# A first search in three rounds in place of four, with 128 thresholds in the first and their comparisons on GpSimd

## The chip, the core and the metric

The kernel runs on one core of a Trainium2 chip. The engines are TensorE (PE, and PEld for its weight loads), VectorE (DVE), ScalarE (ACT), GpSimd (POOL) and SyncE (SP, which issues DMAs here). Each takes its instructions in the order of the program, and they wait for each other by semaphores. The metric is the device time of one execution in microseconds (us), the median of several runs.

## The reference, cut to what matters

Pooled attention (keys and values are means over 8 tokens), then a mixture of eight experts in which each expert takes at most `cap` = 576 of the 4608 tokens, given out in the order of the gate logits over all pairs of token and expert.

```python
scores = scale * np.matmul(q, k_p.transpose(0, 1, 3, 2))      # k_p, v_p: means over 8
attn = softmax(scores)
x = (attn @ v_p)                                              # as 4608 tokens x 512
logits = x @ w_gate                                           # 8 experts
for idx in np.argsort(-logits.flatten()):
    tok, e = idx // E, idx % E
    if assigned[tok] >= 0 or counts[e] >= cap:
        continue
    assigned[tok] = e
    counts[e] += 1
for e in range(E):
    out[assigned == e] = np.maximum(x[assigned == e] @ w1[e], 0) @ w2[e]
```

## The kernel before

The 4608 tokens are 36 tiles of 128 (`NC` = 36, one token in each partition). Three stages follow each other.

**Attention** (`Attention.run`) loops over the tiles with a pipeline: iteration n makes the score products of tile n (`st_s`), turns the weights of tile n - 1 (`st_e`), multiplies tile n - 2 with the values (`st_av`), and on DVE takes the maximum of tile n (`top`), subtracts it (`softmax`, ACT then takes the exponent), and normalises tile n - 3 (`norm`). The bank of the score products is there once, so the score products of tile n + 1 wait for the subtraction of tile n. The gate logits come out of the same value products (`gates`): every fourth `norm` adds the heads of four tiles into `lg` with one longer reduction. A batch has 4.5 tiles; two iterations in each batch have a `prep_v` and a `prep_g` more. GpSimd pools k and v of batches 1 to 7 (`pool_k`, `pool_v`). `after[i]` is a list of steps that are put behind norm(i), in iteration i + 3; all queues keep the written order. `finish` takes the last three tiles; its `next(after)` calls run `Routing.begin`, which handles the last logits and starts the search.

**Routing** (`Routing`) finds for each of eight phases the expert that fills up next and its tokens. Each token has a best logit `bv` and a one-hot `oh` of its expert. A search narrows a threshold: a round compares the place of every token's best logit with `J` = 32 levels, PE counts for each level and expert how many tokens lie above (36 products of 128 x 8, where four tiles of 32 columns share the weights), DVE tests whether a count is over `cap`, and a product with ones gives every partition the number of levels (`up`), from which the next, 28.4 times finer, places follow. The first search (`search_first`) has four rounds. Its range comes from `bounds`, from the first 24 tiles: per partition a maximum and a minimum, a transpose, a product, and seven small DVE instructions; `best(0, 28)`, `levels`, `place` and the first comparisons follow in iterations 31 to 35. `wanted` gives each token its expert's number in the shadow of the later rounds. `close` makes the expert's number (`eid`) and the row numbers (`rows`) out of the last vote.

**Experts** (`experts`): SP loads the weights of expert `eid`, POOL gathers its rows of x by indirect DMA, ACT and DVE cut both into a high and a low part, PE multiplies. The later searches are laid between these products by due times written into the code. `warm` keeps PE busy with products of ones before the first expert. `wake` is an indirect DMA with no use for its result. If an exact count was missed, `suspect` sets a flag, and all experts run a second time.

Of the kernel before, what the change touches and what calls it, by code (L numbers as in the profile page):

```python
# [9 lines left out]
F32 = mybir.dt.float32  # L10
# [13 lines left out]
class Attention:  # L24
# [44 lines left out]
    def local(self, loc, full, consts, more, then):  # L69
# [12 lines left out]
        n = 0  # L82
# [32 lines left out]
        more()  # L115
# [89 lines left out]
    def prep_g(self, b):  # L205
# [10 lines left out]
        return put  # L216

# [113 lines left out]
    def run(self, ctx, full, consts, more, after, end, warm):  # L331
# [37 lines left out]
        self.local(ctx.enter_context(tc.tile_pool(name="loc", bufs=1)), full, consts, more, first_k)  # L369
# [10 lines left out]
        for n in range(nt):  # L380
# [42 lines left out]
class Routing:  # L423
# [25 lines left out]
    def consts(self, jp, ident):  # L449
# [10 lines left out]
        self.jrow = cst.tile([128, J], F16, name="jrow")  # L460
# [20 lines left out]
        nc.gpsimd.tensor_scalar(self.untri, self.tri, -31.0, None, op0=OP.mult)  # L481
        self.spread = cst.tile([128, 224], F16, name="spread")
# [6 lines left out]
    def more(self):  # L489
# [14 lines left out]
        self.q2 = cst.tile([128, NC, 2], F16, name="q2a")  # L504
        self.cmp = cst.tile([128, NC + 3, J], BF, name="cmp")
        self.thr = cst.tile([128, J], F32, name="thr")
        self.lg0 = cst.tile([128, NC, 8], F32, name="lg0")
        self.lo0 = cst.tile([128, 1], F32, name="lo0")
# [5 lines left out]
    def before_search(self, n):  # L514
# [6 lines left out]
        else:  # L521
            for g in self.g0:
                nc.scalar.activation(g[:1], self.ones[:1, :16], AF.Copy, scale=-1.0 - EDGE)
            nc.scalar.activation(self.jrow, self.i36[:, :self.J], AF.Copy)
# [18 lines left out]
    def bounds(self, wk, cols):  # L543

        nc = self.nc
        lg = self.lg[:, :cols].rearrange("p c e -> p (c e)")
        mm = wk.tile([128, 2], F32, name="mm")
        nc.vector.tensor_reduce(mm[:, 0:1], lg, axis=AX.X, op=OP.max)
        nc.vector.tensor_reduce(mm[:, 1:2], lg, axis=AX.X, op=OP.min)
        nc.vector.tensor_scalar(mm[:, 1:2], mm[:, 1:2], -1.0, None, op0=OP.mult)  # L550
        yield
        ps = self.psum()
        nc.tensor.transpose(ps[:2, :128], mm, self.ident)
        m2 = wk.tile([2, 1], F32, name="m2")
        nc.vector.tensor_reduce(m2, ps[:2, :128], axis=AX.X, op=OP.max)
        d2 = wk.tile([2, 2], F32, name="d2")
        nc.vector.tensor_scalar(d2, self.ident[:2, :2], m2, None, op0=OP.mult)
        one = wk.tile([2, 128], F32, name="one2")
        nc.vector.memset(one, 1.0)
        yield  # L560
        ps = self.psum()
        nc.tensor.matmul(ps[:, :2], one, d2, start=True, stop=True)
        b = wk.tile([128, 3], F32, name="b2")
        nc.vector.tensor_copy(b[:, :2], ps[:, :2])

        nc.vector.tensor_tensor(b[:, 2:3], b[:, 0:1], b[:, 1:2], op=OP.add)
        nc.vector.scalar_tensor_tensor(self.hi, b[:, 2:3], 0.125, b[:, 0:1], op0=OP.mult, op1=OP.add)
        nc.vector.scalar_tensor_tensor(self.lo0, b[:, 2:3], -0.125, b[:, 1:2], op0=OP.mult, op1=OP.subtract)
        self.ranges()
# [6 lines left out]
    def place(self, c0, c1):  # L576

        if c0 == 0:
            self.q32 = self.wk.tile([128, self.NC], F32, name="q32")
        self.nc.vector.tensor_scalar(self.q32[:, c0:c1], self.bv[:, c0:c1], self.lo0, self.scale, op0=OP.subtract,  # L580
                                     op1=OP.mult)

    def one(self, c):

        nc = self.nc
# [5 lines left out]
    def best(self, c0=0, c1=None):  # L591
# [3 lines left out]
        if c0 == 0:  # L595
            n = self.n = 1 - getattr(self, "n", 1)
            self.bv, self.oh = self.bvs[n], self.ohs[n]
# [1051 lines left out]
```

## Time and profile before

| | |
|---|---|
| median of three runs | 596.1 us (595.87 to 596.28) |
| profiled execution, its own time | 595.69 us |
| its span, first to last instruction | 593.9 us |
| PE busy | 572.0 us (96%) |
| DVE busy | 392.6 us (66%) |
| ACT busy | 304.7 us (51%) |
| POOL busy | 180.4 us (30%) |
| mean granted clock of PE | 0.983 |

The times of the rows are microseconds from the start of the span. "Busy" is the union of an engine's instructions. Matmul ends are modelled, so a PE that shows 100% need not be at its peak; a row's idle time is that of its engine just before it, with what ended it. Spans on POOL are rough.

### The profile page before, as it was taken

To read this page: it belongs to the slowest core of one execution; us is meant where nothing else is said; L and a number is where in the kernel's file an instruction comes from. 1 tells how busy PE (TensorE), PEld (TensorE's weight loads), DVE (VectorE), ACT (ScalarE), POOL (GpSimd) and SP (SyncE) were. 2 spreads that over 40 slices of the span, in tenths; PEclk is the share of its full clock that TensorE was granted. 3 is DMA by queue.
4 is the path that set the end of the run, shared out by engine and by line. 5 is a ranking of instruction groups with operands and counts; after the bars stand their busy time and mean duration, and the time that the engine had idled before them with its cause. 6 is when DMAs were issued, how large, how long until landed. Compare 5 with 4: busy or idle time off the path is not lost.

```text
span 593.9 us, 11073 instructions
## 1 busy us (share of the span) xinstructions
PE 572.0 (96%) x4045; PEld 506.9 (85%) x4045; DVE 392.6 (66%) x1139; ACT 304.7 (51%) x631; POOL 180.4 (30%) x235
## 2 busy tenths in 40 slices
PE   7999999995999999999999999999999999999993
PEld 4999999993897799779978987997899899889972
DVE  8677887997886778668766876586487346416200
ACT  6444444452551385376745584285549627935210
POOL 3999999200200410330222121112221212210021
PEclk9999999995999999999999999999999999999997
DMA  8999982113541763547538337543833653350010
GB/s 347 419 424 420 423 309 90 72 72 113 165 143 37 256 196 130 136 108 293 98 97 283 102 79 224 165 108 74 273 124 81 200 190 89 89 195 12 2 58 26
DMA packets 64016, 99.83 MB, mean 168 GB/s; under 512 B 34752, under 2 KB 34768, under 8 KB 61392
## 3 DMA queue, kind: packets, MB, share of 16 engines
q1 hardware_dynamic: 52704, 70.66, 35.3%
q0 software_dynamic: 5920, 18.89, 10.0%
q10 hardware_dynamic: 5328, 9.48, 4.2%
q8 instruction: 34, 0.56, 0.4%
q14 instruction: 30, 0.25, 0.1%
HBM read 72.40 MB, written 18.87 MB: 154 GB/s over the span
## 4 chain that ended last, share of the span: by engine, by line
PE 85%; issue 7%; DVE 4%; DMA 2%; POOL 1%; ACT 0%; another core or an unknown queue 0%; POOLq 0%; SPq 0%; ACTq 0%; DVEq 0%
PE h L1215 32%; PE h L1251 27%; PE psa L269 7%; PE pss L224 6%; PE h L1256 4%; PE pse L256 2%; PE rt L256 1%; DMA rawq<-in_q_dram 1%; PE rt L662 1%; DMA out_dram<-yt,rows 1%; PE rt L210 1%; PE rt L714 1%; DVE e L238 1%; PE h L535 1%; PE tp L1188 1%
## 5 line engine op out<-in xcount | busy, mean ns | idle before, releaser
L1251 PE MATMUL h<-w2h,hh 128*128 128x512 f32 x256 | 101.9, 398 | 0.3 <-PEq L1332 0.3
L1251 PE MATMUL h<-w2h,hl 128*128 128x512 f32 x256 | 101.3, 396 | 0.0
L1251 PE MATMUL h<-w2l,hh 128*128 128x512 f32 x256 | 101.0, 394 | 0.0
L1231 POOL DMA_INDIRECT out_dram<-yt,rows x36 | 38.0, 1056 | 195.9 <-ACT yt L1271 170.0
L1220 ACT ACTIVATE hh<-h 128x256 fp32r<-128x256 f32 (+2 forms) x129 | 52.6, 409 | 83.6 <-PE h L1215 83.2
L1215 PE MATMUL h<-xh,w1h 128*128 128x256 f32 (+2 forms) x516 | 93.4, 299 | 0.2 <-ACT xh L1190 0.2
L1215 PE MATMUL h<-xl,w1h 128*128 128x256 f32 (+2 forms) x516 | 91.9, 298 | 0.0
L1215 PE MATMUL h<-xh,w1l 128*128 128x256 f32 (+2 forms) x516 | 90.6, 296 | 0.0
L1215 PEld LDWEIGHTS h<-xh,w1h 128*128 128x128 f32 x516 | 76.9, 189 | 1.2 <-ACT xh L1190 0.5
L1215 PEld LDWEIGHTS h<-xl,w1h 128*128 128x128 f32 x516 | 76.3, 190 | 0.1
L1215 PEld LDWEIGHTS h<-xh,w1l 128*128 128x128 f32 x516 | 76.1, 189 | 0.0
L1119 POOL DMA_INDIRECT xa<-xd,rows x33 | 33.3, 1009 | 135.3 <-ACT xg L1142 38.8
L1225 DVE SCALAR_TENSOR_TENSOR hl<-h,hh 128x256 fp32r<-128x256 f32 (+2 forms) x129 | 56.8, 448 | 21.5 <-ACT hl L1223 10.9
L1271 ACT ACTIVATE yt<-h 128x512 f32<-128x512 f32 x32 | 19.1, 597 | 93.5 <-PE h L1251 79.9
L269 PE MATMUL psa<-vblk,eT 128*128 128x146 f32 (+3 forms) x390 | 59.2, 302 | 0.1
L1251 PEld LDWEIGHTS h<-w2h,hh 128*128 128x128 f32 x256 | 48.2, 188 | 9.3 <-issue 0.7
L1251 PEld LDWEIGHTS h<-w2l,hh 128*128 128x128 f32 x256 | 48.2, 188 | 9.2
L1251 PEld LDWEIGHTS h<-w2h,hl 128*128 128x128 f32 x256 | 48.3, 189 | 8.4
L1168 DVE TENSOR_TENSOR w1l<-raw,w1h 128x512 fp32r<-128x512 f32 x64 | 42.0, 686 | 17.7 <-ACT w1h L1164 17.5
L269 PEld LDWEIGHTS psa<-vblk,eT 128*128 128x128 f32 (+1 forms) x390 | 50.7, 179 | 1.5 <-issue 0.3
L1177 DVE TENSOR_TENSOR w2l<-raw,w2h 128x512 fp32r<-128x512 f32 x64 | 43.2, 682 | 3.4 <-ACT w2h L1174 3.1
L224 PE MATMUL pss<-kblk,rawq 128*128 128x144 f32 (+1 forms) x320 | 43.4, 293 | 1.9 <-PE psa L201 0.9
(253 smaller groups left out, 942.9 us busy)
## 6 DMA issues: line engine op xcount, KB each, us to landing
raw<-in_moe_w_dram SPq DMA_DIRECT2D x64, 512.0 KB, 6.0
xd<-xt ACTq DMA_DIRECT2D x36, 256.0 KB, 6.2
rawv<-in_v_dram SPq DMA_DIRECT2D x7, 1280.0 KB, 12.8
rawk<-in_k_dram SPq DMA_DIRECT2D x7, 1152.0 KB, 12.7
rawq<-in_q_dram SPq DMA_DIRECT2D x6, 1152.0 KB, 11.9
rawq<-in_q_dram SPq DMA_DIRECT2D x2, 640.0 KB, 11.0
rawk<-in_k_dram SPq DMA_DIRECT2D x2, 576.0 KB, 3.9
rawq<-in_q_dram SPq DMA_DIRECT2D x2, 512.0 KB, 6.2
```

What stands on the lines that cost most here:

```text
L224: nc.tensor.matmul(ps[cols, j // 2, 144 * (j % 2):144 * (j % 2) + 144], self.q_of(b, j, n, cols.stop - cols.start), self.kblk[b % 4][:, j] ...
L269: self.nc.tensor.matmul(o[h], self.eT[i][:, c, h], self.vblk[b % 4][:, self.BLOCKS[c]:self.BLOCKS[c + 1]], start=(c == cs[0]), stop=(c == ...
L1119: self.nc.gpsimd.indirect_dma_start(out=to[:n], out_offset=None, in_=self.xd, in_offset=bass.IndirectOffsetOnAxis(ap=rows[:n, t:t + 1], ax ...
L1168: self.nc.vector.tensor_tensor(l, raw, h.bitcast(F32), op=OP.subtract)
L1177: self.nc.vector.tensor_tensor(self.w2l[:, i], self.raw2[e][:, i], self.w2h[:, i].bitcast(F32), op=OP.subtract)
L1215: nc.tensor.matmul(ps[:, :m], a[:, j, fs], b[:, j, o], start=(n == 0), stop=(n == 11))
L1220: nc.scalar.activation(hh[:, f, o], ps[:, :m], AF.Relu)
L1225: later(0.65, 0.4, lambda f=f, o=o, m=m, ps=ps: nc.vector.scalar_tensor_tensor(hl[:, f, o], ps[:, :m], 0.0, hh[:, f, o].bitcast(F32), op0= ...
L1231: st = nc.gpsimd.indirect_dma_start(out=rows, out_offset=bass.IndirectOffsetOnAxis(ap=idx, axis=0), in_=y, in_offset=None)
L1251: nc.tensor.matmul(ps, a[:, f, o], b[:, f], start=(f == 0 and k == 0), stop=(f == 7 and k == 2))
L1256: nc.tensor.matmul(ps, self.hl[:, f, 512:], b[:, f], start=(f == 0 and k == 0), stop=(f == 7 and k == 1))
L1271: self.nc.scalar.activation(y, ps, AF.Copy)
```

## The change

- **Range** (`mix`, `range_of`): from the first 16 tiles, out of the largest logit, the smallest and the smallest best logit. A 4 x 7 matrix of constants (built on GpSimd in `more`) gives, by one product, the lower ends, the three step sizes and the places' origin at once; ACT makes the copies. Its steps stand behind norm(15), norm(16), norm(18) and norm(27), its transpose and its product behind the score products of iterations 20 and 24 (`mid`).
- **First round with 128 thresholds**: `thr` holds 128 levels. GpSimd compares 32 tiles, one `tensor_scalar` of 128 columns for each (`compare`), into a tile in one of the four buffers of `rawq` (`room`), and makes the one-hot rows of these tiles (`fresh`, 8 columns each), the places of 32 tiles (`place`) and the products with the expert numbers (`wish`). DVE takes the best logits of these tiles (`top_of`), and all of the last four tiles (`late_tiles`).
- **Rounds 2 and 3** are as before, with 32 levels; the fourth is gone. `wanted` is no longer run for the first search: the last four tiles of `wish` go under the second round, the reduction under the third.
- `wake` and `levels` (now on GpSimd) stand behind norm(22), the comparisons behind norm(23), norm(27) and norm(31).

```diff
-    def run(self, ctx, full, consts, more, after, end, warm):
+    def run(self, ctx, R, consts, more, after, mid, end, warm):
...
             if n in behind:
                 behind[n]()
+            for f in mid.get(n, ()):
+                f()
...
-        self.jrow = cst.tile([128, J], F16, name="jrow")
+        self.jrow = cst.tile([128, 128], F16, name="jrow")
...
+        nc.gpsimd.tensor_scalar(self.jrow, jp, self.pcol, None, op0=OP.add)
...
+    def mix(self, loc):
...
+        sh = [0.3125 * (J * SHRINK) ** -i / J for i in range(3)]
...
+        for r, row in enumerate(rows):
+            for c, x in enumerate(row):
+                if x:
+                    nc.gpsimd.memset(t[:, c, r:r + 1], x)
...
+    def range_of(self, i, n=16):
...
+        if i == 0:
+            self.n = 0
+            self.bv, self.oh = self.bvs[0], self.ohs[0]
+            nc.vector.tensor_reduce(self.mixed, self.mixt, axis=AX.X, op=OP.add)
+            nc.vector.tensor_reduce(self.mm[:, 0:1], lg, axis=AX.X, op=OP.max)
+            nc.vector.tensor_reduce(self.mm[:, 1:2], lg, axis=AX.X, op=OP.min)
+        elif i == 1:
+            self.top_of(0, n)
+            nc.vector.tensor_reduce(self.mm[:, 2:3], self.bv[:, :n], axis=AX.X, op=OP.min)
+        elif i == 2:
+            ps = self.psum()
+            nc.tensor.transpose(ps[:4, :128], self.mm, self.ident)
+            self.m4 = wk.tile([4, 128], F32, name="m4")
+            nc.scalar.activation(self.m4, ps[:4, :128], AF.Copy, scale=self.mixed[:, 6:7])
+        elif i == 3:
+            m = wk.tile([4, 1], F32, name="m1")
+            nc.vector.tensor_reduce(m, self.m4, axis=AX.X, op=OP.max)
+            self.d4 = wk.tile([4, 6], F32, name="d4")
+            nc.scalar.activation(self.d4, self.mixed[:, :6], AF.Copy, scale=m)
+        elif i == 4:
+            ps = self.psum()
+            nc.tensor.matmul(ps[:, :6], self.one4, self.d4, start=True, stop=True)
+            b = self.cst.tile([128, 6], F32, name="b6")
+            nc.scalar.activation(b, ps[:, :6], AF.Copy)
+            self.lo0, self.lo1, self.steps1, self.los = b[:, 0:1], b[:, 1:2], b[:, 2:5], b[:, 5:6]
+        elif i == 5:
+            self.scale1 = wk.tile([128, 1], F32, name="scale1")
+            nc.vector.reciprocal(self.scale1, self.steps1[:, 0:1])
...
-        self.nc.vector.tensor_scalar(self.thr, self.i36[:, :self.J], self.steps[:, 0:1], self.lo0, op0=OP.mult,
-                                     op1=OP.add)
...
+        self.nc.gpsimd.tensor_scalar(self.thr, self.jrow, self.steps1[:, 0:1], self.lo1, op0=OP.mult, op1=OP.add)
...
+    def wish(self, c0, c1, eng=None):
+
+        (eng or self.nc.vector).tensor_tensor(self.ow[:, c0:c1], self.oh[:, c0:c1],
+                                              self.wtb[:, None, :].to_broadcast([128, c1 - c0, 8]), op=OP.mult)
+
+    def fresh(self, c0, c1):
+
+        for c in range(c0, c1):
+            self.nc.gpsimd.tensor_scalar(self.oh[:, c], self.lg[:, c], self.bv[:, c:c + 1], None, op0=OP.is_equal)
+
+    def compare(self, c0, c1):
+
+        if c0 == 0:
+            self.cmp0 = self.room()
+        for c in range(c0, c1):
+            self.nc.gpsimd.tensor_scalar(self.cmp0[:, c], self.thr, self.bv[:, c:c + 1], None, op0=OP.is_lt)
+
+    def late_tiles(self, c0, c1):
+
+        nc, n = self.nc, c1 - c0
+        bv = self.bv[:, c0:c1]
+        nc.vector.tensor_reduce(bv, self.lg[:, c0:c1], axis=AX.X, op=OP.max)
+        nc.vector.tensor_tensor(self.cmp0[:, c0:c1], self.thr[:, None].to_broadcast([128, n, 128]),
+                                bv[:, :, None].to_broadcast([128, n, 128]), op=OP.is_lt)
+        nc.vector.tensor_tensor(self.oh[:, c0:c1], self.lg[:, c0:c1], bv[:, :, None].to_broadcast([128, n, 8]),
+                                op=OP.is_equal)
...
+        ps = self.psum()
+        count(0, NC - 1, lambda c: self.cmp0[:, c])
+        yield 0
+        up = self.bank("pse")[:, :1]
+        self.place(NC - 4, NC)
+        count(NC - 1, NC, lambda c: self.cmp0[:, c])
+        test(0, self.gz)
+        nc.tensor.matmul(up, self.ones, self.gz, start=True, stop=True)
+        for k in (1, 2):
+            q2 = wk.tile([128, NC, 2], F16, name="q2")
+            finer(q2, self.q32[:, :, None].to_broadcast([128, NC, 2]))
+            compare(0, 4, 12, 24, NC)
+            if k == 1:
+                q32 = wk.tile([128, NC], F32, name="q32")
+                finer(q32, self.q32)
+                self.q32 = wk.tile([128, NC], F32, name="q32c")
+                nc.vector.tensor_scalar(self.q32, q32, -34.0, 66.0, op0=OP.max, op1=OP.min)
+            lower(k - 1)
+            if k == 1:
+                self.wish(NC - 4, NC)
             else:
...
+                self.want = wk.tile([128, NC], F32, name="want")
+                nc.vector.tensor_reduce(self.want, self.ow, axis=AX.X, op=OP.max)
...
-        self.best(self.NC - 8, self.NC - 2)
+        NC = self.NC
+        self.late_tiles(NC - 4, NC - 2)
+        yield
+        self.late_tiles(NC - 2, NC - 1)
         next(g)
         yield
...
+        self.late_tiles(NC - 1, NC)
...
-        A.run(c2, R.ones, lambda: R.consts(A.jp, A.ident), R.more, {NC - 16: [lambda: R.before_search(1)], NC - 14: [lambda: R.before_search(0)], NC - 11: [step], NC - 10: [step], NC - 9: [step], NC - 8: [lambda: R.best(0, NC - 8)],
-                                                       NC - 7: [start], NC - 6: [start, lambda: wake(nc, R, rwk, moe_w2)],
-                                                       NC - 5: [R.levels], NC - 4: [lambda: R.place(0, NC - 8)]},
+        f = lambda f, *a: [lambda: f(*a)]
+        A.run(c2, R, lambda: R.consts(A.jp, A.ident), R.more, {
+            15: f(R.range_of, 0), 16: f(R.range_of, 1), 18: f(R.range_of, 3), 19: f(R.before_search, 0),
+            20: f(R.before_search, 1), 22: f(wake, nc, R, rwk, moe_w2) + f(R.levels),
+            23: f(R.top_of, 16, 24) + f(R.compare, 0, 24) + f(R.fresh, 0, 24),
+            24: f(R.wish, 0, 24, nc.gpsimd),
+            27: f(R.range_of, 5) + f(R.top_of, 24, 28) + f(R.compare, 24, 28) + f(R.fresh, 24, 28) + f(R.place, 0, 28, nc.gpsimd),
+            31: f(R.top_of, 28, 32) + f(R.compare, 28, 32) + f(R.fresh, 28, 32) + f(R.place, 28, 32, nc.gpsimd)
+            + f(R.wish, 24, 32, nc.gpsimd)}, {20: f(R.range_of, 2), 24: f(R.range_of, 4)},
```

## Rows read from the trace of the kernel before

**Rows 1.** The stages: for each stretch (us from the start of the span) its length, then for each engine the busy us and in brackets the number of instructions, the granted clock of TensorE, the busy share of the DMA engines and GB/s.

```profile
134.00:142.00 8.00, 4.74 (x115) 3.86 (x116) 6.53 (x37) 3.26 (x15) 0.31 (x4) 0.64 0.24 88
...
142.00:150.00 8.00, 4.67 (x23) 1.89 (x22) 5.79 (x24) 1.54 (x3) 2.18 (x3) 0.50 0.51 164
...
160.00:300.00 140.00, 140.00 (x998) 122.79 (x997) 107.40 (x343) 77.33 (x158) 26.79 (x35) 1.00 0.50 152
...
300.00:540.00 240.00, 240.00 (x1538) 212.82 (x1537) 145.22 (x418) 139.09 (x265) 48.80 (x70) 1.00 0.48 146
```

**Rows 2.** The timeline of the search: start us, length us, engine, line, operation, output<-input, shapes, count. Rows of one line that follow each other are merged (four comparisons in one row); `over` is the test.

```profile
134.40 0.17 DVE L756 TENSOR_SCALAR_CACHE_REDUCE over<-rt 32x8 bf16<-32x8 f32 x1
...
135.13 0.96 DVE L707 TENSOR_TENSOR cmp<-q,jrow 128x128 bf16<-128x128 f16 x4
...
136.69 0.17 DVE L756 TENSOR_SCALAR_CACHE_REDUCE over<-rt 32x8 bf16<-32x8 f32 x1
...
141.34 0.17 DVE L756 TENSOR_SCALAR_CACHE_REDUCE over<-rt 32x8 bf16<-32x8 f32 x1
```

**Rows 3.** The timeline behind the search, on all engines: the last store of x, the expert's number, the row numbers, the gathers, the first cut of weights, the first cut of rows and the first product. In square brackets: idle time of the engine before the row, and what ended it.

```profile
139.75 0.09 POOL L1125 MEMSET xg<- 1x1 f32 x1 [4.47 <-DMA xd<-xt]
...
142.99 0.14 DVE L796 TENSOR_SCALAR eid<-eid 1x1 int32<-1x1 int32 x1
...
146.76 0.17 DVE L855 TENSOR_SCALAR rows<-found 128x5 int32<-128x5 int16 x1
...
147.21 0.97 POOL L1119 DMA_INDIRECT xg<-xd,rows  x1 [7.38 <-DVE rows L855]
...
148.46 2.31 ACT L1164 ACTIVATE w1h<-raw 128x512 fp32r<-128x512 f32 x4 [10.32 <-DMA raw<-in_moe_w_dram]
...
148.49 0.95 POOL L1119 DMA_INDIRECT xg<-xd,rows  x1 [0.30 <-issue]
...
151.21 0.60 ACT L1190 ACTIVATE xh<-tp 128x512 fp32r<-128x512 f32 x1 [0.45 <-PE tp L1188]
...
151.86 0.66 PE L1215 MATMUL h<-xh,w1h 128*128 128x128 f32 x4 [0.25 <-ACT xh L1190]
```

**Rows 4.** The timeline of TensorE in the attention: the score products of iterations 20, 24, 29 and 33.

```profile
75.39 1.25 PE L224 MATMUL pss<-kblk,rawq 128*128 128x144 f32 x8
...
88.58 1.25 PE L224 MATMUL pss<-kblk,rawq 128*128 128x144 f32 x8
...
104.91 1.25 PE L224 MATMUL pss<-kblk,rawq 128*128 128x144 f32 x8
...
119.19 1.25 PE L224 MATMUL pss<-kblk,rawq 128*128 128x144 f32 x8
```

**Rows 5.** The timeline of TensorE's weight loads: the two products of the range and the score products of iteration 32, with the idle time before them.

```profile
108.12 0.08 PEld L553 LDWEIGHTS rt<-ident,mm 128*2 128x2 f32 x1 [0.25 <-ACT eT L257]
...
111.33 0.29 PEld L562 LDWEIGHTS rt<-d,one 2*128 2x128 f32 x2 [0.25 <-ACT eT L257]
...
115.50 1.03 PEld L224 LDWEIGHTS pss<-kblk,rawq 128*128 128x128 f32 x8 [0.36 <-DVE e L238]
```

**Rows 6.** The timeline of VectorE in the attention: a maximum of a plain iteration and the copy that an iteration with `prep_g` makes, with the idle time before them.

```profile
79.70 0.76 DVE L232 TENSOR_REDUCE mx<-pss 128x8 f32<-128x576 f32 x1 [0.43 <-PE pss L224]
...
86.75 0.25 DVE L213 TENSOR_TENSOR vblk<-rt,mask 128x88 f32<-128x88 f32 x1 [0.71 <-PE rt L210]
```

**Rows 7.** The timeline of VectorE near the end of the attention: the thresholds and the places of 28 tiles.

```profile
126.90 0.29 DVE L573 TENSOR_SCALAR thr<-i,steps,lo 128x32 f32<-128x32 f32 x1
...
129.90 0.30 DVE L580 TENSOR_SCALAR q<-bv,lo,scale 128x28 f32<-128x28 f32 x1
```

**Rows 8.** The timeline of GpSimd: its first instruction of pooled values, the dummy gather of `wake` behind the last pooling, and the next instruction.

```profile
13.21 1.23 POOL L188 TENSOR_TENSOR vblk<-vsum,mask 128x128 f32<-128x128 f32 x3 [8.54 <-DVE vsum L180]
...
107.36 1.09 POOL L1291 DMA_INDIRECT norow<-in_moe_w_dram,ti  x1 [0.17 <-issue]
...
118.56 0.09 POOL L323 MEMSET xt<- 1x1 f32 x1 [10.10 <-DVE mx L232]
```

**Rows 9.** GpSimd's instructions by size. First three rows of its timeline (constants at the start); then rows of the grouping by line and shape: busy us in all and mean ns of one, then the idle time before them.

```profile
3.07 0.57 POOL L481 TENSOR_SCALAR untri<-tri 128x128 bf16<-128x128 bf16 x1
3.69 0.30 POOL L483 MEMSET spread<- 128x224 f16 x1
3.94 0.14 POOL L486 MEMSET g<- 128x16 bf16 x1
...
L178 POOL TENSOR_TENSOR t<-rawv 128x1280 f32<-128x1280 f32 x7 | 20.3, 2903 | 0.5
...
L179 POOL TENSOR_TENSOR t<-t 128x640 f32<-128x640 f32 x7 | 10.8, 1544 | 0.6
...
L188 POOL TENSOR_TENSOR vblk<-vsum,mask 128x128 f32<-128x128 f32 x9 | 3.6, 402 | 9.1 <-DVE vsum L180 8.5
...
L64 POOL IOTA jp<- 128x128 int32 x1 | 0.2, 232 | 0.4 <-POOLq L1636 0.4
```

**Rows 10.** Two lines by themselves: the subtraction of the maximum on VectorE and the first adds of pooling on GpSimd; count, then min/median/max ns and the first and last start in us.

```profile
L238 DVE TENSOR_TENSOR e<-pss,mx x36: 745/758/759, 10.1 to 128.0; 128x576 f32<-128x576 f32 x36
...
L165 POOL TENSOR_TENSOR tk<-rawk x7: 2627/2634/2640, 15.5 to 94.1; 128x1152 f32<-128x1152 f32 x7
```

**Rows 11.** One us of the stages, with the same columns as the first group.

```profile
149.00:150.00 1.00, 1.00 (x4) 0.18 (x2) 0.88 (x2) 1.00 (x3) 0.70 (x2) 0.52 0.76 256
```

More of the change, by code (lines that the diff above doesn't have):

```diff
@@ L114, in local @@
         then()
-        more()
+        more(loc)
     def load_k(self, b, halves=(slice(0, 4),)):
@@ L216, in prep_g, with room @@
         return put
+    def room(self):
+        t = self.raw.tile([128, 4 * self.S], F32, name="rawq", bufs=4)
+        return t.bitcast(BF).rearrange("p (c j) -> p c j", c=self.nt)
     def st_s(self, i):
@@ L541, in late @@
         self.nc.vector.tensor_copy(self.fold[:, :self.J], self.spread[:, 96:128])
[L543 to L569, printed above, removed]
@@ L608, in places, with best @@
+    def best(self):
+        nc, NC = self.nc, self.NC
+        n = self.n = 1 - getattr(self, "n", 1)
+        self.bv, self.oh = self.bvs[n], self.ohs[n]
+        nc.vector.tensor_reduce(self.bv, self.lg, axis=AX.X, op=OP.max)
+        nc.vector.tensor_copy(self.q16, self.places())
+        nc.vector.tensor_tensor(self.oh, self.lg, self.bv[:, :, None].to_broadcast([128, NC, 8]), op=OP.is_equal)
     def places(self):
@@ L724, in finer, with test @@
             nc.vector.tensor_scalar(out, q, up, J * SHRINK, op0=OP.subtract, op1=OP.mult)
-        for k in range(rounds):
-            last = k + 1 == rounds
-            early = 0
-            if k == 0:
-                for c0, c1 in ((0, 16), (16, NC - 8), (NC - 8, NC - 2)):
-                    compare(c0, c1)
-                    yield 0
-                early = NC - 1
-                ps = self.psum()
-                count(0, early)
-                yield 0
-                up = self.bank("pse")[:, :1]
-                self.place(NC - 8, NC)
-            else:
-                compare(0, 4, 12, 24, NC)
-                if not last:
-                    q32 = wk.tile([128, NC], F32, name="q32")
-                    finer(q32, self.q32)
-                    self.q32 = q32
-                if k == 1:
-                    self.q32 = wk.tile([128, NC], F32, name="q32c")
-                    nc.vector.tensor_scalar(self.q32, q32, -34.0, 66.0, op0=OP.max, op1=OP.min)
-                lower(k - 1)
-                if k > 1:
-                    next(shadow, None)
-                ps = self.psum()
-            count(early, NC)
+        def test(p0, g):
+            over = wk.tile([128, 8], BF, name="over")
+            nc.vector.tensor_scalar(over[p0:], ps[p0:, :8], float(self.cap), None, op0=OP.is_gt, op1=OP.max,
+                                    accum_out=g[p0:, 0:1])
@@ L754, in search_first @@
             g = self.g0[k % 2]
[L755 to L758 removed]
+            test(96, g)
+            if k == 2:
                 nc.vector.tensor_scalar(g[96:, 8:], ps[96:, :8], float(self.cap), None, op0=OP.is_ge)
             nc.tensor.matmul(up, self.ones, g[:, :1], start=True, stop=True)
[L761 to L763 removed]
@@ L935, in phase @@
         else:
-            yield from self.search(sh) if k else self.search_first(sh)
+            yield from self.search(sh) if k else self.search_first()
         if k == 0:
```

98 lines of the change are left out of this document (40 added, 58 removed).

## The prediction

> **What bounds the kernel now.** I read the stages first, then the one stage in which TensorE (PE) is not full, then what follows it. From 160 to 540 us PE is busy all the time, but in 134 to 142 us it is busy for 4.74 of 8 us and in 142 to 150 for 4.67 of 8 [rows 1]. Those 16 us are the first search and the way from it to the first expert: whatever they lose or gain moves all of the rest.
>
> In the search, see the period. A round is a test on VectorE (DVE), one product that gives every partition the vote, new places, four comparisons that end at 136.09, 36 small products (one for each tile of tokens), and the next test. The tests start at 134.40, 136.69 and, two rounds on, 141.34: 6.94 us for three rounds, 2.31 each [rows 2]. PE and DVE take turns, so a round is latency alone and nothing runs under it.
>
> From the last vote two chains leave. The expert's number (142.99) leads to the weights, whose first high part is cut at 148.46; the row numbers (146.76) lead to the gather at 147.21, the cut of its rows at 151.21 and the first real product at 151.86 [rows 3]. Both start from the vote. The stores of x, which the gather needs, had all landed at 139.75 (the GpSimd memset that waited for them), 7.5 us ahead of it. So if the vote comes 2 or 3 us earlier, nothing else in these rows is late next.
>
> **The round that goes.** Four rounds become three: -2.31 us, all on the path. In return the second round does the reward product of the last four tiles (`wish`) where its DVE work already ended just ahead of the test: an instruction of 32 columns, about 0.15 us, of which I count 0.1 on the path. The 0.44 us reduction to `want` keeps the place that it has under the last products.
>
> **The range, moved.** Before, it is worked out in iterations 28 to 30 and costs time there. Nine iterations make two batches of attention, so iterations 20 to 24 and 29 to 33 are alike: the score products of 20 and 24 start 13.19 us apart, those of 29 and 33 14.28 us apart [rows 4]. Of these 1.09 us three rows show about 0.86: PE waits 0.25 us twice for the bank that ScalarE (ACT) is emptying, and 0.36 us for the subtraction on DVE, which stood behind the seven small range instructions [rows 5]. All this goes. The new range costs less on DVE (six reductions and a reciprocal, spread over iterations 18 to 30) but falls on a loop with little room: the score products wait for the subtraction of the tile before, and DVE is idle 0.43 us before a maximum in a plain iteration and 0.71 before a `prep_g` [rows 6]. Three reductions after norm(15), some 0.7 us, meet that 0.71; two after norm(16) meet 0.43; `top_of` after norm(23), 0.2 us, meets no idle time, since every fourth norm has a longer reduction. Both products of the range now stand behind the score products, where the bank is already empty. I count 0.2 to 0.3 us lost, bounds 0 and 0.7: net -0.8 us (-0.4 to -1.1).
>
> **DVE at the end.** `levels` (0.29) and the places of 28 columns (0.30) leave DVE in the last two iterations, where it runs back to back [rows 7]. The late comparisons are 128 columns wide in place of 32, about 0.1 us more each for the last two tiles, and the first is about 0.1 shorter, since its places and its 192 columns go. That leaves -0.1 to -0.2 net. With the attention's 0.8, DVE would let the first test start at about 133.5 in place of 134.40.
>
> **GpSimd (POOL), the new work.** This decides. POOL pools k and v without a pause until 107.4, then issues the 1.09 us dummy gather, and has nothing more to do until the stores land [rows 8]. The change does not touch the pooling, so POOL takes up the new work at 108.75: 107.36, 1.09, and 0.30 of issue, as between two gathers, of which the second starts 1.28 after a first of 0.97 [rows 3, 8]. Queued there: the thresholds (0.62), 24 comparisons, 24 `fresh`, `wish` of 192 columns (0.59 by the line through the tensor_tensor rows, 0.187 + 2.12 ns a column [rows 9]), 4 and 4, places (0.2), 4 and 4. With X us from one comparison to the next and Y for a `fresh`, the last `fresh` ends at P = 110.2 + 32 (X + Y). The counts on PE need it, and the test starts 0.3 after it.
>
> No row shows this instruction with a scalar from memory. Nearest for X: a tensor_scalar of 128 columns, `untri`, in 0.57 [rows 9]; ends 0.40 (the 128-column tensor_tensor, two inputs) and 0.62 (from `untri` to the next start). For Y the ends are 0.04 above nothing and 0.57, if the 0.57 does not depend on the columns at all. I take the fixed 0.187 of the tensor_tensor rows, the only family with several sizes, and 8/128 of the remaining 0.39: 0.21. Like memsets start 0.05 before the end of the last (3.69 + 0.30 against 3.94), a memset behind a tensor_scalar 0.05 after it [rows 9]. 64 like, independent instructions are nearer to the first: I take 0.03 off each. X + Y = 0.54 + 0.18 = 0.72, P = 133.2, and the test can start at 133.5: POOL and DVE end together. With the plain durations (0.78) P is 135.2 and the test at 135.5.
>
> The constants' work on POOL (one 128-column instruction, some 25 small memsets) is hidden by its wait from 4.7 to 13.2 us, in which the trace shows no POOL row [rows 8]; without that cover it would cost some 2 us. `wake` keeps its place behind the pooling.
>
> **Sum.** First test 134.40 to 133.5: -0.9. Round: -2.31. `wish`: +0.1. Together -3.1; I take -2.8, since POOL, put at the very point where it ends with DVE, can only move this term up. The profiled execution took 595.69 us around its span of 593.9; the median is 596.1. Forecast 596.1 - 2.8 = 593.3 us.
>
> **Rivals.** *POOL is late (slower).* If most of the 0.57 is the instruction's own cost, Y is large. POOL's iota writes 128 columns in 0.23 in all [rows 9]; if a tensor_scalar streams no slower, at least 0.34 of the 0.57 is fixed, Y is 0.36, X + Y 0.93, P = 140.0 and the test at 140.3: +5.9 - 2.2 = +3.7, 599.8 us. With nothing but fixed cost (1.14) it is 606. The point from which it decides: P = 136.2, X + Y = 0.81; above it the kernel is slower than before. For: an operand of f32 and a scalar from memory are read on top. Against: POOL's tensor_tensor shows 0.187 fixed.
>
> The Trainium skill, GPSIMD Engine Reference, Performance versus the Vector engine, gives about 1.8 cycles an element at 1.2 GHz as the best of a one-input loop. By that estimate 0.19 of the 0.57 is streaming, Y is 0.39 and the time about 600.8: this rival. The same page (When to use GPSIMD) advises against plain elementwise work there; no run here shows the rate yet.
>
> *Break-even.* X + Y of 0.78 to 0.86 gives 595.0 to 597.3. DVE's late comparisons may also meet POOL's: a DVE instruction with two inputs from SBUF beside a POOL one that reads it. The rows show only pairs that do not disturb each other: the subtraction (one input from PSUM) took 745 to 759 ns in all 36 tiles, POOL busy or not, and POOL's adds 2627 to 2640 [rows 10]. The Trainium skill, SBUF — State Buffer, on the shared port pair, has a two-input DVE instruction block against a GpSimd read; these rows neither confirm nor refute it. Six such instructions at up to 0.57 each would add 1 to 3 us if POOL still runs then, which turns the forecast into this case.
>
> *POOL is early.* With X + Y under 0.65 DVE alone sets the test, and the attention's whole 1.1 comes back: -3.4, 592.7.
>
> *The clock.* PE's granted clock stood at its lower level (1.2 GHz) through the search's end and rose at the end of the us from 149 to 150 (0.52 on average [rows 11]), some 1.9 us ahead of the first real product at 151.86, with the warm-up products before it. If the rise does not move with the vote, the products from about 148.9 on run some 1.1 us at half speed: about +0.5, inside the range.
>
> *It does not do what it says.* Three rounds split the range 128 x 28.4 x 28.4 ways, about 1.5e-7; the values on both sides of the first cut are 6.7e-6 apart in these inputs, so the exact second path stays unused. Under 1 in 100.
>
> **How the numbers follow.** The forecast with POOL in time or a little late (592.9 to 595.0) has 0.36, POOL early 0.15, break-even 0.15, POOL late 0.34. Faster by over 0.2% (1.2 us, about what a measurement of this kernel tells from no change) 0.51, within it 0.15, slower 0.34. The range reaches from 592.5 into the slower rival up to 601.0 and leaves out 0.14, most of it POOL with X + Y over 0.96; the likeliest case's own is 592.7 to 595.0.
>
> **What would show it.** Tests 2.31 us apart, now three. Score products of iterations 29 and 33 about 13.2 us apart. POOL: the start-to-start of the comparisons (0.54 here) and of `fresh` (0.18), and the end of the last `fresh` against 133.2. If PE's 32nd count waits for POOL, and not for DVE, beyond 136, I am wrong by that row; if the late comparisons on DVE are well over 0.4 us, contention is why.

## The result and the profile after

| | before | after |
|---|---|---|
| median, lowest to highest (7 runs each) | 596.1 (595.87 to 596.99) | 598.72 (598.1 to 601.18) |
| profiled execution, its span | 595.69, 593.9 | 598.1, 596.3 |
| start of the tests | 134.40, 136.69, (one more), 141.34 | 138.14, 140.53, 142.86 |
| last of GpSimd's comparisons (a `fresh`) ends | (not on GpSimd) | 137.76 |
| first product of the first expert | 151.86 | 153.63 |

The medians are 2.6 us apart; the ratio, taken over all runs, is 1.0051, with a 95% interval of 1.0034 to 1.0067. So the change made the kernel slower by about 2.6 us, where 2.8 us less were forecast. The sign is that of the rival "POOL is late", the size lies between its 599.8 and the break-even case.

GpSimd's timeline in the kernel after, from the dummy gather to its last comparison (start, length, line, operation, output<-input, count):

```profile
107.24 1.09 POOL L1329 DMA_INDIRECT norow<-in_moe_w_dram,ti  x1 [0.18 <-issue]
108.40 0.44 POOL L609 TENSOR_SCALAR thr<-jrow,b 128x128 f32<-128x128 f16 x1
108.94 13.89 POOL L633 TENSOR_SCALAR rawq<-thr,bv 128x128 bf16<-128x128 f32 x24
122.81 6.77 POOL L626 TENSOR_SCALAR oh<-lg,bv 128x8 bf16<-128x8 f32 x24
129.66 0.51 POOL L620 TENSOR_TENSOR ow<-oh,wtb 128x192 bf16<-128x192 bf16 x1
130.15 2.54 POOL L633 TENSOR_SCALAR rawq<-thr,bv 128x128 bf16<-128x128 f32 x4
132.66 1.20 POOL L626 TENSOR_SCALAR oh<-lg,bv 128x8 bf16<-128x8 f32 x4
133.86 0.47 POOL L615 TENSOR_SCALAR q<-bv,b,scale 128x28 f32<-128x28 f32 x1
134.30 2.34 POOL L633 TENSOR_SCALAR rawq<-thr,bv 128x128 bf16<-128x128 f32 x4
136.61 1.15 POOL L626 TENSOR_SCALAR oh<-lg,bv 128x8 bf16<-128x8 f32 x4
```

There is no gap over 0.1 us in it: GpSimd works from 108.40 to 137.76. The 24 comparisons give X = 13.89 / 24 = 0.579, the 24 `fresh` Y = 6.77 / 24 = 0.282, so X + Y = 0.861, and the prediction's formula with these gives P = 110.2 + 32 x 0.861 = 137.75; the row ends at 137.76. The form of the term was right, its price was not.

Who waits for it: TensorE's timeline of the first count, then VectorE's of its last tile and of the tests (answering to [rows 2]):

```profile
133.92 0.17 PE L760 MATMUL rt<-oh,rawq 128*128 128x8 bf16 x1 [0.17 <-POOL oh L626]
136.97 1.12 PE L760 MATMUL rt<-oh,rawq 128*128 128x8 bf16 x8 [2.89 <-POOL oh L626]
```

```profile
133.40 0.29 DVE L640 TENSOR_TENSOR rawq<-thr,bv 128x128 bf16<-128x128 f32 x1
133.61 0.16 DVE L642 TENSOR_TENSOR oh<-lg,bv 128x8 bf16<-128x8 f32 x1
133.68 0.28 DVE L615 TENSOR_SCALAR q<-bv,b,scale 128x4 f32<-128x4 f32 x1
138.14 0.17 DVE L773 TENSOR_SCALAR_CACHE_REDUCE over<-rt 128x8 bf16<-128x8 f32 x1 [4.18 <-PE rt L760]
...
140.53 0.17 DVE L773 TENSOR_SCALAR_CACHE_REDUCE over<-rt 32x8 bf16<-32x8 f32 x1
...
142.86 0.17 DVE L773 TENSOR_SCALAR_CACHE_REDUCE over<-rt 32x8 bf16<-32x8 f32 x1
```

VectorE is done with the last tile's comparison at 133.69 and with its places at 133.96, then stands idle for 4.18 us; TensorE waits 2.89 us for GpSimd. That is the row that the prediction named as the one to make it wrong. The rounds are 2.39 and 2.33 us long.

Behind the search (answering to [rows 3]), the timeline of all engines:

```profile
144.51 0.14 DVE L834 TENSOR_SCALAR eid<-eid 1x1 int32<-1x1 int32 x1
...
148.28 0.17 DVE L893 TENSOR_SCALAR rows<-found 128x5 int32<-128x5 int16 x1
148.74 1.05 POOL L1157 DMA_INDIRECT xg<-xd,rows  x1 [5.62 <-DVE rows L893]
...
152.98 0.60 ACT L1228 ACTIVATE xh<-tp 128x512 fp32r<-128x512 f32 x1 [0.35 <-PE tp L1226]
153.63 0.66 PE L1253 MATMUL h<-xh,w1h 128*128 128x128 f32 x4 [0.25 <-issue]
```

The last test, the expert's number and the row numbers are each 1.52 us later than before; the cut and the first product 1.77. Another 0.4 us comes in the first expert's second stage, where TensorE waits for gathered rows of the next expert (experiment 8).

The attention, TensorE's timeline of the score products of iterations 20, 21, 24, 25, 29 and 33 (answering to [rows 4]), then the weight load and the product of the range's first step:

```profile
75.28 1.25 PE L229 MATMUL pss<-kblk,rawq 128*128 128x144 f32 x8
78.78 1.14 PE L229 MATMUL pss<-kblk,rawq 128*128 128x144 f32 x8
...
88.84 1.25 PE L229 MATMUL pss<-kblk,rawq 128*128 128x144 f32 x8
92.61 1.25 PE L229 MATMUL pss<-kblk,rawq 128*128 128x144 f32 x8
...
105.63 1.25 PE L229 MATMUL pss<-kblk,rawq 128*128 128x144 f32 x8
...
118.82 1.25 PE L229 MATMUL pss<-kblk,rawq 128*128 128x144 f32 x8
```

```profile
76.71 0.08 PEld L586 LDWEIGHTS rt<-ident,mm 128*4 128x4 f32 x1 [0.40 <-issue]
76.74 0.27 PE L586 MATMUL rt<-ident,mm 128*4 128x128 f32 x1 [0.21 <-DVE mm L583]
```

29 to 33 takes 13.19 us, just what the prediction said. But 20 to 24 takes 13.56 in place of 13.19, and 24 to 25 3.77, where the trace of before has 3.25: about 0.9 us (0.37 and 0.52) are paid where the two products of the range went, and not 0.2 to 0.3. At iteration 33 the kernel after is 0.37 us ahead of before (118.82 against 119.19 [rows 4]), not 0.8.

### The profile page after: what moved, and what is told of

It is laid out like the page before. It is cut to its first block, busy times and chain, and to the rows that moved or that the text cites. A ratio compares the mean times of both kernels' runs of the same rounds, so it can differ in the third digit from the quotient of the medians.

```text
span 596.3 us, 11076 instructions
## 1 busy us (share of the span) xinstructions
PE 572.2 (96%) x4008; PEld 506.4 (85%) x4008; DVE 388.6 (65%) x1119; ACT 305.4 (51%) x633; POOL 213.0 (36%) x329
## 4 chain that ended last, share of the span: by engine, by line
PE 73%; POOL 11%; issue 7%; DMA 4%; DVE 2%; POOLq 0%; another core or an unknown queue 0%; ACT 0%; DVEq 0%; ACTq 0%
PE h L1253 32%; PE h L1289 26%; PE h L1294 4%; POOL rawq L633 3%; PE psa L274 3%; PE pss L229 3%; DMA rawq<-in_q_dram 2%; POOL oh L626 2%; POOL t L178 1%; PE rt L708 1%; POOL tk L165 1%; POOL vblk L188 1%; POOL kblk L169 1%; POOL t L179 1%; PE pse L261 1%
```

## The experiments

The theory: GpSimd's 64 instructions set the test, and they are dear because each reads its scalar from memory. Rivals: the columns cost more than thought, the kind of output counts, or contention with VectorE stretches them. Beside that: once GpSimd is out of the way, does VectorE end at 133.5?

**1. GpSimd's price by itself.** Kernel of before, with seven groups of four instructions on scratch data behind `wake`, where GpSimd has nothing to do.

```diff
+        x = s[:, 5:6]
+        for i in range(4):
+            g.tensor_scalar(self.prb[:, i], s, x, None, op0=OP.is_lt)
+        for i in range(4):
+            g.tensor_scalar(self.prb[:, i, :8], s[:, :8], x, None, op0=OP.is_equal)
+        for i in range(4):
+            g.tensor_scalar(self.prb[:, i], s, 0.5, None, op0=OP.is_lt)
...
```

> The kernel before with 28 extra GpSimd instructions on scratch tiles behind wake, where GpSimd is idle from 108.5 us on; the results are not used. Groups of four: comparison of 128 columns with a scalar from memory to bf16; the same of 8 columns; both with a constant in place of the scalar; 128 columns to f32 and to f16; 64 columns to bf16. Theory A (fixed cost of the instruction, no matter where the scalar is): 128 columns 0.58 us from start to start, 8 columns 0.28, 64 columns 0.42, constants the same. Theory B (the scalar from memory costs it): with a constant 0.1 us or more less in both widths. Theory C (the bf16 output costs it): to f32 or f16 0.1 us or more less at 128 columns. The kernel's own time should stay within 0.5 us of the kernel before, since the stores that GpSimd's next instruction waits for land later than the probe ends.

It took 596.54 us. GpSimd's timeline of it: scalar from memory with 128 and 8 columns, constant scalar with 128 and 8, output f32, output f16, 64 columns:

```profile
107.99 2.36 POOL L336 TENSOR_SCALAR prb<-prs 128x128 bf16<-128x128 f32 x4
110.34 1.15 POOL L338 TENSOR_SCALAR prb<-prs 128x8 bf16<-128x8 f32 x4
111.47 2.01 POOL L340 TENSOR_SCALAR prb<-prs 128x128 bf16<-128x128 f32 x4
113.45 0.82 POOL L342 TENSOR_SCALAR prb<-prs 128x8 bf16<-128x8 f32 x4
114.26 2.34 POOL L344 TENSOR_SCALAR prf<-prs 128x128 f32<-128x128 f32 x4
116.58 2.37 POOL L346 TENSOR_SCALAR prh<-prs 128x128 f16<-128x128 f32 x4
118.93 1.72 POOL L348 TENSOR_SCALAR prb<-prs 128x64 bf16<-128x64 f32 x4
```

From group to group, by four: 0.588 against 0.495 with 128 columns, 0.283 against 0.203 with 8. So the scalar from memory costs 0.08 to 0.09 us each time, a column 2.5 ns ((0.588 - 0.283) / 120), and what is left, about 0.18, is fixed. Output f32 or f16 makes no difference (0.580, 0.588). The theory of the scalar holds, with a difference a little under the 0.1 us that was set for it; that of the output falls. A column costs no more than thought (the prediction had 0.39 us for 128 of them, 3 ns each). Contention with VectorE is small here: of the groups of four comparisons in the kernel after, one took 2.54 us beside VectorE's own comparison and the other 2.34. With constants X + Y would have been 0.495 + 0.203 = 0.70, P = 132.6 by the formula: the 0.72 of the prediction was a fair price for another instruction.

**2. `fresh` taken from GpSimd** (kernel after, one VectorE instruction for each group of 24, 4 and 4 tiles).

```diff
-        for c in range(c0, c1):
-            self.nc.gpsimd.tensor_scalar(self.oh[:, c], self.lg[:, c], self.bv[:, c:c + 1], None, op0=OP.is_equal)
+        self.nc.vector.tensor_tensor(self.oh[:, c0:c1], self.lg[:, c0:c1],
+                                     self.bv[:, c0:c1, None].to_broadcast([128, c1 - c0, 8]), op=OP.is_equal)
```

> The changed kernel with one part undone: the one-hot rows of the first 32 tiles are made by VectorE, one two-input instruction for each group of 24, 4 and 4 tiles, in place of 32 small instructions on GpSimd. Theory (GpSimd's queue sets the first test: 32 comparisons at 0.58 us and 32 fresh at 0.28 us end at 137.76, and the test stands at 138.14): GpSimd's last comparison ends 32 x 0.28 = 9 us earlier, near 129, VectorE's late tiles set the test near 133.5 to 134, so the time falls by 4 to 4.6 us against the changed kernel, to 594.0 to 594.8, which is 1.3 to 2.1 us under the kernel before. Rival (the moved range, the wider late comparisons and latency behind the search cost the time, and GpSimd only happens to end last): the test moves by 1 us at most, 597.5 to 598.7.

599.96 us, ratio 1.0064 (1.0051 to 1.0076). GpSimd's last comparison now ends at 131.83, yet the test starts at 136.93. The timeline of both engines and of the score products' weight loads near iteration 27:

```profile
99.83 2.89 POOL L178 TENSOR_TENSOR t<-rawv 128x1280 f32<-128x1280 f32 x1
...
100.19 2.76 DVE L625 TENSOR_TENSOR oh<-lg,bv 128x192 bf16<-128x192 f32 x1
...
104.53 1.03 PEld L229 LDWEIGHTS pss<-kblk,rawq 128*128 128x128 f32 x8 [2.62 <-DVE e L243]
```

The comparison of 192 columns needs about 0.36 us (experiment 3), and here 2.76: it starts inside GpSimd's add and ends 0.23 us behind it (102.95 against 102.72). TensorE stands idle for 2.62 us ahead of the score product behind it. GpSimd no longer set the test, but the 594.0 to 594.8 us that were expected did not come: a wait of another kind had taken its place. Five of six runs took 599.7 to 600.2 and the traced one 596.89; a second trace of the same code (experiment 9) showed the same wait. Where the other 3 us of those five runs lie, no trace shows.

**3. The range's products elsewhere** (experiment 2, and the two products put into iterations 21 and 25).

```diff
-            + f(R.wish, 24, 32, nc.gpsimd)}, {20: f(R.range_of, 2), 24: f(R.range_of, 4)},
+            + f(R.wish, 24, 32, nc.gpsimd)}, {21: f(R.range_of, 2), 25: f(R.range_of, 4)},
```

> As the kernel with the one-hot rows on VectorE, and the two products of the range one iteration later (behind the score products of iterations 21 and 25 in place of 20 and 24). In the changed kernel the steps from iteration 20 to 21 and from 24 to 25 took 3.50 and 3.77 us, 0.45 and 0.52 more than the like steps of the kernel before. Theory (in 20 the transpose waits for a maximum on VectorE that has just been made, in 24 the product and its copy stand before the turned weights of an iteration that turns both halves first): both shrink by 0.2 us or more, 0.4 to 0.8 us in all, so 0.4 to 0.8 us under the kernel with the one-hot rows on VectorE. Rival (the products cost this wherever they stand, since TensorE is full): the same 0.9 to 1.0 us in other iterations, and no difference of time over 0.3 us.

594.6 us, ratio 0.9988 (0.9967 to 1.0008; ten runs at 594.1 to 594.9, two at about 600). Score products 20 to 21 are 3.05 apart, 24 to 25 3.19, but 25 to 26 3.52: the first product's cost is nearly gone, the second's only moved. The larger part came by luck of the order, in the timeline of the same place as above:

```profile
99.91 0.36 DVE L625 TENSOR_TENSOR oh<-lg,bv 128x192 bf16<-128x192 f32 x1
99.95 3.08 POOL L178 TENSOR_TENSOR t<-rawv 128x1280 f32<-128x1280 f32 x1
```

Here VectorE was ahead by 0.04 us, took 0.36, and GpSimd's add took 3.08 in place of 2.89. The test is at 134.41.

**4. Four tiles fewer for GpSimd** (kernel after, tiles 28 to 31 on VectorE).

```diff
-            31: f(R.top_of, 28, 32) + f(R.compare, 28, 32) + f(R.fresh, 28, 32) + f(R.place, 28, 32, nc.gpsimd)
+            31: f(R.late_tiles, 28, 32) + f(R.place, 28, 32)
```

> The changed kernel with the tiles 28 to 31 taken off GpSimd: VectorE makes their best logits, comparisons (one instruction of 512 columns), one-hot rows and places in iteration 34. Theory (GpSimd's queue sets the first test): the last GpSimd row that the counts need ends near 133.9 as tile 27's did, the test stands at 134.2 to 134.8 and the time falls by 3.3 to 3.9 us to 594.8 to 595.4, less than with the one-hot rows on VectorE. Rival (GpSimd is not what decides): no gain, or a loss of the 0.9 us that VectorE does more at its busy end.

595.85 us, ratio 0.9998 (0.9989 to 1.0007): 2.9 us less than after, for four comparisons and four `fresh` fewer, 3.4 us by the prices above. GpSimd's last `fresh` ends at 134.29, 3.47 earlier than after; the test is at 135.06, behind VectorE's last tile (134.81). The two end within 0.6 us of each other, and the kernel ties with before: 0.3 us later at the test and 0.45 us longer than the upper ends that were expected. Its last test (139.79) is 1.55 us earlier than before's, and yet its span is that of before, 593.9 us; the part on the prediction comes back to this.

**5. The wait taken away by order** (experiment 3, with one comparison of 28 tiles behind iteration 28, when GpSimd's pooling is over).

```diff
-            23: f(R.top_of, 16, 24) + f(R.compare, 0, 24) + f(R.fresh, 0, 24),
-            24: f(R.wish, 0, 24, nc.gpsimd),
+            23: f(R.top_of, 16, 24) + f(R.compare, 0, 24),
...
+            28: f(R.fresh, 0, 28) + f(R.wish, 0, 24, nc.gpsimd),
```

> As the kernel with the one-hot rows on VectorE and the range's products one iteration later, but the 28 one-hot rows are made by one VectorE instruction behind norm(28), when GpSimd is at its comparisons of 0.6 us, in place of behind norm(23), when it is at an add of 2.9 us. Theory (a VectorE instruction with two inputs from SBUF waits for the end of a GpSimd instruction that began before it; behind norm(23) it took 2.76 us in one trace and 0.36 in another): it can wait 0.6 us at most, and all runs lie together at 594.0 to 594.9, none near 597 or 600. Rival (the spread comes from elsewhere, the gathers or the stores): some runs near 600 stay.

593.79 us (593.38 to 594.25), before on that chip 595.46: ratio 0.997 (0.9958 to 0.9982), faster than both kernels. VectorE's timeline:

```profile
115.51 0.43 DVE L625 TENSOR_TENSOR oh<-lg,bv 128x224 bf16<-128x224 f32 x1
...
134.00 0.17 DVE L773 TENSOR_SCALAR_CACHE_REDUCE over<-rt 128x8 bf16<-128x8 f32 x1
...
138.72 0.17 DVE L773 TENSOR_SCALAR_CACHE_REDUCE over<-rt 32x8 bf16<-32x8 f32 x1
```

The same comparison, 32 columns wider, takes 0.43; GpSimd's last comparison ends at 128.89 and VectorE alone sets the test, at 134.00. All six runs lie together, a little below the range that was expected, and none is near 600.

**6 and 7. Is it the two inputs?** Kernel of before, with twelve VectorE instructions of 192 columns beside the pooling, once with two inputs from SBUF (the first line below, experiment 6) and once, at the same places, with one (the second, experiment 7).

```diff
+        self.nc.vector.tensor_tensor(self.prb, x, self.pr[:, :24, None].to_broadcast([128, 24, 8]), op=OP.is_equal)
+        self.nc.vector.tensor_reduce(self.prm, x, axis=AX.X, op=OP.max)
```

> The kernel before with one VectorE comparison of 192 columns with two inputs from SBUF, on scratch tiles, behind each of norm(6) to norm(17), while GpSimd pools without a pause; its result is not used. Theory (it waits for the GpSimd instruction that began before it): its 12 durations spread from 0.36 to 3 us, each long one ends with a GpSimd row, and the attention gets longer by the sum, some 8 to 15 us less what is idle. Rival (no such wait; the long row had another cause): all 12 near 0.36 us and the time 1 to 3 us longer.

> The same places, but a VectorE reduction over 192 columns with one input from SBUF. Theory: all 12 last the same, about 0.34 us, whatever GpSimd does, and the time is 1 to 3 us longer than the kernel before. Rival (any VectorE access to SBUF waits for GpSimd): the durations spread as with two inputs.

603.64 against 595.97 us, one run each; before took 595.46 on that chip, so twelve instructions with one input cost 0.5 us, where 1 to 3 were expected. The probe's line by itself (count, shortest/median/longest ns, first and last start), in 6 and then in 7, and a piece of the timeline of 6:

```profile
L333 DVE TENSOR_TENSOR prb<-prs x12: 345/798/3072, 41.9 to 86.6; 128x192 bf16<-128x192 f32 x12
```

```profile
L333 DVE TENSOR_REDUCE prm<-prs x12: 333/342/347, 41.9 to 79.4; 128x24 f32<-128x192 f32 x12
```

```profile
47.49 2.89 POOL L182 TENSOR_TENSOR t<-rawv 128x1280 f32<-128x1280 f32 x1
47.63 2.96 DVE L333 TENSOR_TENSOR prb<-prs 128x192 bf16<-128x192 f32 x1
...
53.00 0.35 DVE L333 TENSOR_TENSOR prb<-prs 128x192 bf16<-128x192 f32 x1
53.01 1.86 POOL L192 TENSOR_TENSOR vblk<-vsum,mask 128x128 f32<-128x128 f32 x3
```

With one input it hardly varies. With two, nine of the twelve end 0.21 to 0.22 us behind the end of the GpSimd instruction that was running when they began; the one at 53.00, which began just ahead of GpSimd's, and two more beside a like row of three took 0.34 to 0.35. The two probes differ in their operation and output too, but [rows 10] leave little room for that as the cause: there a TENSOR_TENSOR that writes 576 columns, with one of its inputs in PSUM, took 745 to 759 ns in all 36 tiles, beside the same pooling. The Trainium skill, SBUF — State Buffer, "SBUF: two separate sides", says that whichever of the two engines starts first holds the shared ports for its whole instruction, and counts a VectorE instruction with two SBUF inputs in. These runs agree: 345 to 3072 ns against 333 to 347.

**8. Only the range's products moved** (kernel after, the diff of experiment 3 alone).

> The changed kernel with only the two products of the range one iteration later. With the one-hot rows on VectorE this move goes with the loss of some 0.4 us of attention. Theory (GpSimd's queue sets the first test, and it does not depend on the attention's pace): the attention ends 0.3 to 0.5 us earlier, the test stays at 138.0 to 138.3 and the time the same within 0.5 us of the changed kernel, 598.2 to 599.2. Rival (attention and test are coupled): 0.4 us or more faster.

599.54 us, ratio 1.0074 (1.0059 to 1.0089). The attention is 0.2 us shorter (score product of iteration 35 at 124.93, after 125.13), but the test stands at 137.97, 0.17 earlier, since GpSimd still sets it. By the test alone the kernel should have been 0.2 faster than after; it was not, and it missed the 598.2 to 599.2 us that were expected. The timeline of TensorE, at the second cut of the next expert's rows:

```profile
204.86 0.66 PE L1226 MATMUL tp<-ident,xg 128*128 128x128 f32 x4 [1.72 <-DMA xg<-xd,rows]
```

The first gather of these rows was issued at 198.91; the row follows 5.95 us later. In the kernel after it is 4.41 us (198.88 to 203.29, a wait of 0.20), in before 4.04 without a wait (197.07 to 201.11). So the same gather costs the path 0 to 1.7 us, and in the traces that hides the 0.2 gained. Why it lands later in one kernel than in another was not tried.

**9 and 10. Second traces** of the code of experiments 2 and 3, to find their longer times.

> The same code as the second experiment's, for a trace of one of its longer times (599.7 to 600.2 in five of six runs, 596.9 in the traced one). If the extra 3 us are a second wait of one DVE instruction with two inputs from SBUF for POOL's adds, one of DVE's fresh, comparison or wish rows shows 1 to 3 us here that took under 0.7 in the first trace, and the test starts about 3 us later than 136.93. If they are the gather of expert 1's rows landing late, the test stands at 136.9 and TensorE waits 1 to 3 us for the gathered rows ahead of the second cut, in expert 0's second stage. At 596.9 again it says nothing.

> The same code as the third experiment's, whose times were 594.1 to 594.9 in ten runs and about 600.0 in two. At about 600: the comparison of 192 columns ahead of iteration 27 now starts behind POOL's add of 1280 columns and takes about 2.9 us in place of 0.36, the test starts 2.5 to 3 us later than 134.41, and the rest is a wait for a gather (theory: two inputs from SBUF against POOL). At about 594.5 the comparison took 0.36 again.

Both fell on their shorter times, 597.1 and 594.21, and say nothing of the longer ones. They repeat the wait (2.76 us, test at 137.12) and its absence (0.36, test at 134.18).

## Why the prediction was wrong, by its own steps

- **GpSimd's price (X + Y = 0.72): the step that failed.** Measured 0.861. The probe gives 0.70 with constants, so the rest is the scalar from memory, 0.08 to 0.09 on each of 64 instructions. That price turned "POOL and DVE end together" into a wait of 2.89 us for GpSimd, and the sign of the forecast with it. The text said "no row shows this instruction with a scalar from memory", listed the operand under the rival's "for", and yet took a value without it. The 0.03 taken off each "like, independent" instruction was too much as well: with the scalar from memory the probe's instructions last 0.596 and 0.297 us and start 0.588 and 0.283 apart, so 0.01 is saved. That 0.72 comes so near the 0.70 of constants is partly luck: X was put too high for them (0.54 against 0.495) and Y too low (0.18 against 0.203).
- **P = 110.2 + 32 (X + Y), the test 0.3 behind it, and the point X + Y = 0.81:** right. 137.75 against 137.76, the test 0.38 later. The agreement to 0.01 is luck: the rest of the queue came out 0.3 us shorter than the 110.2 holds, and the last eight pairs took 0.90 in place of 0.861. At 0.861 this working gives a test at 138.05 and, at +3.65 - 2.2, a kernel slower by about 1.5 us; the last vote is 1.52 later. (For the break-even case the text has 597.3 at 0.86; its own sum gives 597.5.) Experiment 4 is the same rule from the other side.
- **The round, -2.31:** right. Three rounds at 2.39 and 2.33 in place of four give -2.22 with `wish` in them.
- **The attention, -0.8: mis-sized.** The 1.09 us at iterations 29 to 33 came back in full, but the new places cost about 0.9 where 0.2 to 0.3 were counted, and 0.37 were left of the 0.8. The reductions up to iteration 20 cost nothing (it starts at 75.28, before at 75.39 [rows 4]). What I had priced at nothing ("behind the score products, where the bank is already empty") were the products themselves: in 20 the first waits 0.40 us, of which TensorE's row gives 0.21 to a minimum on VectorE that had just been made, and in 24 ScalarE copies the second (0.18) ahead of `eT`, which the iteration's other products need. Experiment 3 shows the first cost go and the second follow its product. VectorE would have let the test start at 134.0 to 134.4 (experiments 5 and 3), not 133.5. So with GpSimd on time the kernel would have been faster, but by less: experiment 5 is 1.67 us under before, where 2.8 were forecast.
- **Contention:** not in the kernel after. Its late comparisons took 0.43 with 256 columns and 0.29 with 128, beside a GpSimd that never paused. The wait is real (6 and 7), but its size goes with what GpSimd runs: in the pooling VectorE's instruction lasted up to 2.7 us longer, while beside GpSimd's comparisons the rows show 0.2 at most (the 32 columns of experiment 3: 0.41 beside them, 0.19 in a pause of GpSimd).
- **The clock:** in the kernel after the rival falls. The granted clock was 0.50 (the lower level) from 150 to 151 and 0.95 from 151 to 152, so it rose at about 151.1, 1.1 us later than before [rows 11], with a vote 1.52 later, and 1.2 us ahead of the first transposes of gathered rows. In four experiments it comes back. In experiment 5 the vote was 2.62 us earlier than before, but the clock rose at about 149.1, only 0.9 earlier, and these transposes stood ahead of the rise: they took 1.09 us in place of 0.63, close to the +0.5 that the prediction gave this rival. In experiments 3, 4 and 8 they took 1.00, 1.06 and 0.91. Why the rise did not follow the vote there is not shown.

The stages of the kernel after, with the same columns as [rows 1], and one us of experiment 5:

```profile
150.00:151.00 1.00, 1.00 (x4) 0.42 (x3) 0.00 (x0) 0.56 (x2) 0.90 (x1) 0.50 0.92 270
151.00:152.00 1.00, 0.56 (x3) 0.00 (x0) 0.90 (x2) 1.00 (x3) 0.70 (x2) 0.95 0.86 242
```

```profile
149.00:150.00 1.00, 0.78 (x5) 0.36 (x4) 0.78 (x2) 0.60 (x1) 0.82 (x1) 0.95 0.52 135
```

TensorE's timeline of the first transposes, before, after and in experiment 5:

```profile
150.54 0.63 PE L1188 MATMUL tp<-ident,xg 128*128 128x128 f32 x4 [0.32 <-issue]
```

```profile
152.31 0.63 PE L1226 MATMUL tp<-ident,xg 128*128 128x128 f32 x4 [0.75 <-issue]
```

```profile
148.07 1.09 PE L1226 MATMUL tp<-ident,xg 128*128 128x128 f32 x4 [0.35 <-issue]
```

- **Beyond the vote: a term put at nothing.** The prediction let all that the vote gains or loses reach the end ("nothing else in these rows is late next"). The kernel after lost 0.25 us more at the first gather and 0.4 at the next expert's, with smaller losses later, which make +1.52 into the +2.4 of the spans. An earlier vote, the prediction's own case, was not kept in full either. In experiment 5 the first expert's number is 2.63 us earlier than before, the second's 1.98 (187.55 against 189.53), the last one's 1.65, and the span 1.6. Of the first 0.65 lost, the transposes at the lower clock are 0.46 and a later landing of the first gather 0.16. In experiments 3 and 4 the vote was 2.20 and 1.55 us earlier and the span 1.0 and 0.0 shorter. So 0.9 to 1.5 us were missing from the sum here. That the same rows land later in some kernels stays open.

## What to carry to other kernels

A queue of 64 small instructions multiplies every 0.1 us of doubt by 64: when no row shows the very form, with a scalar from memory as against a constant, price the form at the upper of its bounds, or forecast the side on which most of the bounds lie. Where the plan makes two engines end together, only lateness can happen; ask for the distance to the decision point (here 0.09 of 0.81) before the sign. And before moving an elementwise comparison to VectorE, look at what GpSimd reads at that moment: an instruction of 0.36 us can last as long as GpSimd's. A gain in one stage has to be followed to the end of the kernel: of a vote 2.6 us earlier, 1.6 us were left.

## What the runs showed of the hardware

A GpSimd tensor_scalar of 128 partitions cost about 0.18 us, 2.5 ns for each column, and 0.08 to 0.09 more where its scalar came from memory; its output's type did not matter. The prediction's estimate from the Trainium skill, GPSIMD Engine Reference, Performance versus the Vector engine, gave Y = 0.39; measured 0.282, between that and the 0.18 forecast.

A VectorE comparison of 192 columns with two SBUF inputs, 0.35 us by itself, lasted 2.46 to 3.07 us when it started 0.04 to 0.39 us behind a GpSimd add of 2.6 to 2.9 us, and went unhindered when it was 0.01 to 0.04 us ahead of it: which of the two engines was first moved the test by 2.5 us (136.93 in experiment 2, 134.41 in experiment 3).
